# First product of a state-space block with an MLP: two units at a time in seven block products, the scan cut into small pieces between them

## Chip, cores and metric

The kernel runs on one core of one Trainium2 chip. The metric is the device time in microseconds of one execution of the whole program; the time of a version is the median of several executions. Engines are named as in the profile: PE (TensorE matmul), PEld (its weight loads), DVE (VectorE), ACT (ScalarE), POOL (GpSimd), SP (SyncE, which only issues DMAs here).

## What is computed

A Mamba-2 scan over 4 batches, 8 heads, 768 positions, head size 32 and state size 16, and behind it, per token, a two-layer MLP with Silu. The reference, cut:

```python
log_a = np.log(np.clip(a, 1e-06, 1.0))
for c in range(nc):                                   # chunks in time
    L = np.exp(cum[..., :, None] - cum[..., None, :]) * causal
    M = np.einsum('bhin,bhjn->bhij', Cc, Bc) * L
    y = np.einsum('bhij,bhjd->bhid', M, xc) + np.einsum('bhin,bhnd->bhid', Cc, state) * np.exp(cum)
    state = decay_full * state + np.sum(Bx * decay_from_j, axis=2)
x = y.transpose(0, 2, 1, 3).reshape(3072, 256)
h = x @ w_in                                          # 3072x256 by 256x2048
out = (h / (1 + exp(-h))) @ w_out                     # 3072x2048 by 2048x256
```

Everything is fp32, except that the two weight matrices arrive as 64-bit floats and are converted on the chip.

## The kernel before, in words

**Units.** The 3072 tokens are 12 units of 256 (UT), three per batch. Each unit goes through the scan, then the first product (`f_s1`), then the second (`f_s2`).

**The scan of a unit** is a chain of pieces. `f_P` (L237) clips the decays of the unit and scans them on DVE (tile pfx); `f_E` (L264) does the same for the 64-by-64 decay table E, one DVE scan over 1024 columns. `f_T` (L277) transposes B and C on PE into a PSUM tile and ACT copies them out (bh, and ce twice with masks); `f_C` (L294) multiplies C by pfx on DVE (cw); `f_B` (L271) multiplies B by E's last column, on POOL in the loop (BT). `f_G` (L297) runs the small matmuls of the chunk states and of C by B into the four PSUM banks of tile gy; DVE multiplies by E (M), then ACT copies the states out (dm). `f_S` (L334) chains the states on DVE (st). `f_Y` (L352) runs the small matmuls of y into gy again, and ACT copies them to XM, the transposed input of the MLP.

**The first product**, `f_s1(g, j)`, j from 0 to 7, makes two of the 16 feature blocks: four block products of 128x128 weights by 128x256 tokens into one PSUM bank (tile hp, two buffers), and one Silu over 512 columns on ACT into gT. **The second product**, `f_s2(g, j)`, makes four products for half c = j // 4 of the unit's output rows into tile o_ps (two buffers); after 16 of them ACT copies the half out and SP stores it in two DMAs. Every block product stands in the trace as two PE records, each with its weight load.

**The order** is written out by hand; engines run their own instructions in that order and wait on each other only for data and buffers. In the start (L424 to L486) the scans of units 0 to 2, the conversion of the 16 weight pieces and the first products of units 0 and 1 are interleaved. A piece n is loaded into a ring of 8 raw buffers, `w_size` (ACT), `w_bits` (DVE, then POOL) and `w_sign` (DVE) convert it, and the sign step issues the load of piece n + 8. `busy(n)` (L192) runs n products of zeros on PE. Then the loop (L487) over g = 2 to 13 does in each of eight steps j: four first products of unit g, a piece of the scan of unit g + 1, four second products of unit g - 2. The last two rounds have second products only. `load_unit` puts the loads of a later unit on SP's queue.

Tiles of the scan come from pool `sc` (two buffers each), loads from `loads` (three). PSUM has eight banks: four for gy, two for hp, two for o_ps. Two accesses of different engines to one bank of a tile are put one behind the other.

## Time and profile before

| | us |
|---|---|
| runs shown | 399.66, 400.35, 400.27 |
| median | 400.27 |
| profiled execution, its own time | 399.42 |
| its span, first to last instruction | 397.7 |
| PE busy | 384.8 |
| DVE, ACT, POOL busy | 114.5, 116.1, 32.7 |
| first products (L388), 768 records, busy | 180.9 |
| second products (L399), 768 records, busy | 180.7 |

The span is what the trace shows; 1.72 us of the execution lie around it. "Busy" of PE counts overlapping records once, and matmul ends are modelled, so a cost per product is better read from the chain of waits, where each piece ends when the next begins. In a row of grouped instructions stand line, engine, operation, out<-in, shapes and count, then busy us and mean ns of one, then the idle time of the engine just before them and what ended it. In a row of the timeline stand start and duration in us, and the idle time before in brackets.

### The profile page before, as it was taken

The numbers are of one execution on the slowest core, as the hardware profiler recorded it, in microseconds if no ns is written. First come the engines' busy times: TensorE is split into PE (matmuls) and PEld (weight loads), VectorE is DVE, ScalarE is ACT, GpSimd is POOL, SyncE is SP. The second block draws the span as 40 slices with busy tenths as digits, with TensorE's granted clock in tenths as the row PEclk, the third lists the DMA queues.
The fourth block names the chain that finished last, engine by engine and source line by source line (L and its number), as shares of the span: only waits on it lengthen the run. The fifth ranks groups of instructions, "written<-read, shape, count | busy, mean of one in ns | idle before, by whom it ended". The sixth has DMA issues, their size and how long they took to land.

```text
span 397.7 us, 7960 instructions
## 1 busy us (share of the span) xinstructions
PE 384.8 (97%) x3477; PEld 323.3 (81%) x3477; DVE 114.5 (29%) x211; ACT 116.1 (29%) x250; POOL 32.7 (8%) x38
## 2 busy tenths in 40 slices
PE   8779899999999999999999999999999999999995
PEld 3447788888888888888888888888888888888884
DVE  7763988660600500410420330240150110000000
ACT  2445756223313222322322322321322222221000
POOL 2222356200000000000000000000000000000000
PEclk9899999999999999999999999999999999999999
DMA  9999399405403502601700700900900000000101
GB/s 153 198 283 232 132 191 126 45 2 93 51 5 80 56 16 58 76 15 41 93 15 25 109 15 14 119 15 8 128 13 2 15 13 2 15 13 7 21 13 26
DMA packets 105966, 25.18 MB, mean 63 GB/s; under 512 B 97228, under 2 KB 101836, under 8 KB 105932
## 3 DMA queue, kind: packets, MB, share of 16 engines
q1 hardware_dynamic: 103716, 24.42, 34.5%
q10 hardware_dynamic: 2216, 0.26, 0.5%
q8 instruction: 27, 0.44, 0.5%
q14 instruction: 7, 0.06, 0.1%
HBM read 21.52 MB, written 3.15 MB: 62 GB/s over the span
## 4 chain that ended last, share of the span: by engine, by line
PE 92%; DVE 3%; ACT 1%; DMA 1%; issue 1%; ACTq 0%; DVEq 0%
PE o_ps L399 43%; PE hp L388 40%; PE gy L371 2%; PE gy L317 2%; PE gy L362 2%; DMA bct<-in_B_dram 1%; PE gy L309 1%; PE hp L282 1%; PE hp L195 1%; DVE E L248 1%; DVE w_in_sb L159 1%; DVE wu L151 0%; ACT wu L143 0%; DVE st L348 0%; DVE pa L240 0%
## 5 line engine op out<-in xcount | busy, mean ns | idle before, releaser
L388 PE MATMUL hp<-XM,w_in_sb 128*128 128x256 f32 x768 | 180.9, 380 | 4.3 <-DVE w_in_sb L159 2.0
L399 PE MATMUL o_ps<-w_out_sb,gT 128*128 128x256 f32 x768 | 180.7, 381 | 0.0
L388 PEld LDWEIGHTS hp<-XM,w_in_sb 128*128 128x128 f32 x768 | 145.3, 190 | 26.0 <-DVE w_in_sb L159 2.2
L399 PEld LDWEIGHTS o_ps<-w_out_sb,gT 128*128 128x128 f32 x768 | 143.7, 190 | 20.8 <-issue 1.5
L390 ACT ACTIVATE gT<-hp 128x512 f32<-128x512 f32 x96 | 57.4, 598 | 189.3 <-PE hp L388 189.3
L295 DVE TENSOR_TENSOR cw<-hp,pfx 128x256 f32<-128x256 f32 x12 | 5.1, 424 | 150.7 <-ACT ce L291 150.7
L154 POOL TENSOR_TENSOR wv<-wu,wv 128x512 uint32<-128x512 uint32 x16 | 23.5, 1470 | 44.6 <-DVE wu L153 29.3
L274 POOL TENSOR_TENSOR BT<-bct,E 128x256 f32<-128x256 f32 x10 | 6.6, 658 | 216.8 <-DVE E L248 216.8
L404 ACT ACTIVATE o_sb<-o_ps 128x256 f32<-128x256 f32 x24 | 9.2, 384 | 49.7 <-PE o_ps L399 49.7
L321 DVE TENSOR_TENSOR M<-gy,E 128x1024 f32<-128x1024 f32 x12 | 14.7, 1225 | 29.7 <-PE gy L317 29.7
L248 DVE TENSOR_TENSOR_SCAN E<-ab,diag 128x1024 f32<-128x1024 f32 x10 | 22.9, 2292 | 0.8
L329 ACT ACTIVATE dm<-gy,par 128x64 f32<-128x64 f32 (+1 forms) x48 | 10.9, 311 | 21.4 <-DVE M L321 21.4
L151 DVE TENSOR_SCALAR wu<-wu 128x512 f32<-128x512 f32 x16 | 13.1, 820 | 9.8 <-ACT wu L143 9.8
L348 DVE SCALAR_TENSOR_TENSOR st<-st,pfx,dm 128x64 f32<-128x64 f32 x40 | 12.5, 312 | 6.6 <-ACT dm L329 4.9
L362 PEld LDWEIGHTS gy<-cw,st 32*64 32x64 f32 x352 | 6.6, 135 | 6.6 <-issue 3.3
L195 PE MATMUL hp<-idle 128*128 128x512 bf16 x29 | 9.1, 448 | 1.9 <-DVE idle L190 1.3
L145 ACT ACTIVATE wv<-raw 128x512 f32<-128x512 uint32 x16 | 10.9, 678 | 0.0
L143 ACT ACTIVATE wu<-raw 128x512 f32<-128x512 f32 x16 | 10.8, 678 | 0.0
L371 PE MATMUL gy<-M,xt 64*32 64x64 f32 x768 | 10.6, 231 | 0.0
L362 PE MATMUL gy<-cw,st 32*64 32x64 f32 x352 | 8.4, 229 | 2.2 <-ACT wu L143 1.2
L377 ACT ACTIVATE XM<-gy 128x512 f32<-128x512 f32 x12 | 7.2, 597 | 11.1 <-PE gy L371 11.1
L291 ACT ACTIVATE ce<-hp,par 128x256 f32<-128x256 f32 x24 | 10.1, 480 | 0.0
(45 smaller groups left out, 113.0 us busy)
## 6 DMA issues: line engine op xcount, KB each, us to landing
ab<-in_a_dram SPq DMA_DIRECT2D x40, 128.0 KB
raw<-in_moe_w_in_dram SPq DMA_DIRECT2D x8, 512.0 KB
raw<-in_moe_w_out_dram SPq DMA_DIRECT2D x8, 512.0 KB
xt<-in_x_dram SPq DMA_DIRECT2D x24, 128.0 KB
out_dram<-o_sb SPq DMA_DIRECT2D x48, 64.0 KB
bct<-in_C_dram SPq DMA_DIRECT2D x24, 64.0 KB
pa<-in_a_dram SPq DMA_DIRECT2D x11, 128.0 KB
bct<-in_B_dram SPq DMA_DIRECT2D x22, 64.0 KB
```

The lines of the kernel that those rows point to most:

```text
L145: nc.scalar.activation(v, raw[n][:, :, :, 0], AF.Copy, scale=2.0 ** -51, bias=2.0)
L151: nc.vector.tensor_scalar(out=wu[n], in0=wu[n], scalar1=LEAST, scalar2=MOST, op0=ALU.max, op1=ALU.min)
L154: nc.gpsimd.tensor_tensor(out=v, in0=u, in1=v, op=ALU.add)
L195: nc.tensor.matmul(out=t, lhsT=idle[:, 0:128], rhs=idle, start=True, stop=True)
L248: nc.vector.tensor_tensor_scan(out=E[u][:, k:k + n].rearrange("p k h t -> p (k h t)"), data0=t, data1=diag[:, 0:n * H].rearrange("p g t -> ...
L321: nc.vector.tensor_tensor(out=M[u].rearrange("p k g x -> p g k x"), in0=gram[:, :, 0:256].rearrange("p g (k x) -> p g k x", k=2), in1=E[u] ...
L348: nc.vector.scalar_tensor_tensor(out=o, in0=ST[u][:, t], scalar=PFX[u][:, Q * t + Q - 1:Q * t + Q], in1=dm[:, k, c], op0=ALU.mult, op1=ALU ...
L362: nc.tensor.matmul(out=y[64 * q:64 * q + 64, 2 * w + c, 64 * k:64 * k + 64], lhsT=sp[32 * g:32 * g + 32, t], rhs=cw[32 * g:32 * g + 32, Q ...
L371: nc.tensor.matmul(out=y[32 * q:32 * q + 32, 2 * w + c, 64 * k:64 * k + 64], lhsT=xc[64 * c:64 * c + 64, k, h], rhs=m[64 * c:64 * c + 64, ...
L388: nc.tensor.matmul(out=hp[:, i], lhsT=w_in_sb[:, kc, f * 128:(f + 1) * 128], rhs=xm[:, kc], start=(kc == 0), stop=(kc == KC - 1))
L390: nc.scalar.activation(GTS[g][:, 2 * j:2 * j + 2], hp, AF.Silu)
L399: nc.tensor.matmul(out=OPS[g], lhsT=GTS[g][:, f, 128 * c:128 * c + 128], rhs=w_out_sb[:, f, :], start=(f == 0), stop=(f == NF - 1))
```

## The change

**First products from unit 4 on.** Units 2G and 2G + 1 (G from 2 to 5) and feature blocks 2j and 2j + 1 are taken as a 2-by-2 block product with an inner size of two blocks. That is eight block products; `f_x1` does it in seven, after Strassen in Winograd's form. Four sums of weight blocks (SW) are made once on POOL by `f_SW`, four sums of token blocks (XT) per pair on DVE by `f_XT`; both lie in buffers of the raw ring, which has 7 buffers in place of 8. Three PSUM tiles X, W and Y are used per step (hp, three buffers). X collects P1, then P6, P7 and a fourth product on top of each other; between these ACT copies P1 and U2 out, DVE adds from it into gT, and at last ACT takes Silu of it. DVE does three additions per step, ACT three copies and four Silus of 256 columns. The sums lie in gT and Silu is taken there in place.

**Second products** come from a generator (`s2_list`), one product at a time, two units behind in pairs: 1, 3, 3 and 1 per step between the first products. Both halves of a unit lie in one bank (o_ps, one buffer in place of two); ACT copies them out together, 512 columns, but in the last two units half by half.

**The scan** is cut into smaller functions. From unit 6 on `scan_plan` spreads the scans of the next pair's two units over the eight steps: DVE and ACT pieces go between the additions and Silus of `f_x1`, PE's pieces behind it. E is scanned in four pieces, M in two; BT moves to DVE there. The transposes go to a bank of gy in place of hp. Pool `sc` has one buffer (pfx, st and the copies two).

**The start.** `f_Ab` uses hp and `busy` uses o_ps. One `busy(4)` is gone, two are `busy(3)`; `f_S(0)` comes ahead of the first weight steps; for unit 1 `f_C` comes ahead of `f_B` and both ahead of `w_bits(3)`. Unit 3's round of the loop now holds the scans of units 4 and 5.

```diff
-    rawp = ctx.enter_context(tc.tile_pool(name="rawp", bufs=8))
+    rawp = ctx.enter_context(tc.tile_pool(name="rawp", bufs=7))
-    sc = ctx.enter_context(tc.tile_pool(name="sc", bufs=2))
+    sc = ctx.enter_context(tc.tile_pool(name="sc", bufs=1))
-    ps_h = ctx.enter_context(tc.tile_pool(name="ps_h", bufs=2, space=bass.MemoryType.PSUM))
-    ps_o = ctx.enter_context(tc.tile_pool(name="ps_o", bufs=2, space=bass.MemoryType.PSUM))
+    ps_h = ctx.enter_context(tc.tile_pool(name="ps_h", bufs=3, space=bass.MemoryType.PSUM))
+    ps_o = ctx.enter_context(tc.tile_pool(name="ps_o", bufs=1, space=bass.MemoryType.PSUM))
...
-        tp = ps_h.tile([128, 4, 128], FP32, name="hp")
+        tp = ps_s.tile([128, 4, 512], FP32, name="gy")[:, 0]
...
+    def s2_list(units, apart=False):
+        for g in units:
+            o = ps_o.tile([128, 2, d_model], FP32, name="o_ps")
+            o_sb = opool.tile([128, 2, d_model], FP32, name="o_sb")
+            b, t0 = at(g)
+            for c, f in [(c, f) for c in range(2) for f in range(NF)]:
+                nc.tensor.matmul(out=o[:, c], lhsT=GTS[g][:, f, 128 * c:128 * c + 128], rhs=w_out_sb[:, f, :],
+                                 start=(f == 0), stop=(f == NF - 1), skip_group_check=True)
+                if f == NF - 1 and (apart or c == 1):
+                    cs = slice(c, c + 1) if apart else slice(0, 2)
+                    nc.scalar.activation(o_sb[:, cs], o[:, cs], AF.Copy)
...
+                yield
...
+        a0, a1, op = ((wj[:, 0, 1], wj[:, 1, 1], ALU.add), (SW[0], wj[:, 0, 0], ALU.subtract),
+                      (wj[:, 0, 0], wj[:, 0, 1], ALU.subtract), (wj[:, 1, 0], SW[min(i, 1)], ALU.subtract))[i]
+        nc.gpsimd.tensor_tensor(out=t, in0=a0, in1=a1, op=op)
...
+        a0, a1 = ((b1[:, 0], b0[:, 0]), (b1[:, 1], t[:, 0]), (b1[:, 1], b1[:, 0]), (b0[:, 1], t[:, 1]))[i]
+        nc.vector.tensor_tensor(out=t[:, i], in0=a0, in1=a1, op=ALU.subtract)
...
+    def f_x1(G, j, dve, act):
...
+        X, W, Y = (ps_h.tile([128, 512], FP32, name="hp")[:, 0:UT] for _ in range(3))
...
+        mm(X, wj[:, 0, 0, j], b0[:, 0])
+        p1 = copy("p1", X)
+        mm(W, wj[:, 1, 0, j], b0[:, 1])
+        add(g0[:, 2 * j], W, p1)
+        f_s2(1)
+        mm(Y, SW[0][:, j], t[:, 0])
+        p5 = copy("p5", Y)
+        mm(X, SW[1][:, j], t[:, 1], False)
+        u2 = copy("u2", X)
+        silu(g0[:, 2 * j], g0[:, 2 * j])
+        other(dve, 3)
+        other(act, 3)
+        f_s2(3)
+        mm(X, SW[2][:, j], t[:, 2], False)
+        add(g1[:, 2 * j + 1], X, p5)
+        silu(g1[:, 2 * j + 1], g1[:, 2 * j + 1])
+        f_s2(3)
+        mm(X, wj[:, 1, 1, j], t[:, 3], False)
+        silu(g0[:, 2 * j + 1], X)
+        other(dve, 2)
+        mm(Y, SW[3][:, j], b1[:, 1], False)
+        add(g1[:, 2 * j], Y, u2)
+        silu(g1[:, 2 * j], g1[:, 2 * j])
+        other(dve, 1)
+        other(act, 9)
+        f_s2(1)
...
+            plan[j][0].extend([partial(f_P0, u), partial(f_P1, u), E0[0], E0[1], E1[0], E1[1]])
+            plan[j][2].append(partial(f_T0, u))
+            plan[j + 1][0].extend([E1[2], E1[3], partial(f_C, u), partial(f_B, u, nc.vector)])
+            plan[j + 1][1].extend([partial(f_T1, u), partial(f_T2, u, 0), partial(f_T2, u, 1)])
+            plan[j + 1][2].append(partial(f_G, u))
+            plan[j + 2][0].extend([partial(f_M, u, 0), partial(f_M, u, 1), lambda: None, partial(f_S, u, 0, 2),
+                                   partial(f_S, u, 2, 4)])
+            plan[j + 2][1].extend([partial(f_D, u, 0), partial(f_D, u, 1)])
+            plan[j + 2][2].append(partial(f_Y, u))
+            plan[j + 3][1].append(partial(f_X, u))
...
+    for G in range(2, NU // 2):
+        S2.append(s2_list((2 * G - 2, 2 * G - 1)))
+        plan = scan_plan(G + 1) if G + 1 < NU // 2 else [([], [], []) for _ in range(8)]
+        for j, (dve, act, pe) in enumerate(plan):
+            f_x1(G, j, dve, act)
+            for what in pe:
+                what()
...
+    S2.append(s2_list((NU - 2, NU - 1), True))
+    f_s2(64)
```

## The prediction, made before the result was known

> **What bounds the kernel now.** I read the page from the top: busy times, the 40 slices, the chain that ended last.

> ```profile
> span 397.7 us, 7960 instructions
> PE 384.8 (97%) x3477; PEld 323.3 (81%) x3477; DVE 114.5 (29%) x211; ACT 116.1 (29%) x250; POOL 32.7 (8%) x38
> ...
> PE   8779899999999999999999999999999999999995
> ...
> PE 92%; DVE 3%; ACT 1%; DMA 1%; issue 1%; ACTq 0%; DVEq 0%
> ```

> TensorE is busy from the second slice to the last but one, and 92% of the chain is its work. "Busy" is no proof, so I went to the groups of instructions, shapes kept apart, between 66 and 344 us, where the loop over units runs:

> ```profile
> L399 PE MATMUL o_ps<-w_out_sb,gT 128*128 128x256 f32 x580 | 139.0, 382 | 0.0
> L388 PE MATMUL hp<-XM,w_in_sb 128*128 128x256 f32 x576 | 136.1, 379 | 0.0
> ```

> The last column is idle time before the group: 0.0. Nothing that another engine does is late there. The chain of waits cut to one unit gives the true cost of a product, free of the overlap in "mean ns":

> ```profile
> 158.36 0.44 PE hp L282 x4
> ...
> 162.25 0.38 PE gy L309 x32
> 162.64 0.62 PE gy L317 x32
> 163.26 1.92 PE o_ps L399 x8
> 165.18 1.73 PE hp L388 x8
> ...
> 173.82 0.51 PE gy L362 x24
> 174.32 0.79 PE gy L371 x53
> ...
> 189.12 0.44 PE hp L282 x4
> ```

> Every block product is two records, so eight records are four products: 1.73 / 4 = 0.432 us. The unit repeats after 189.12 - 158.36 = 30.76 us, which is 64 products (27.65) and 3.1 of scan (0.44 + 0.38 + 0.62 + 0.51 + 0.79, and twice 0.19 where 1.92 stands for 1.73). So in the loop time is the count of products, and a product removed is worth 0.432 us as long as no wait takes its place.

> **Term 1, the products.** From unit 4 on, a step of two units does 7 first products instead of 8; 4 pairs x 8 steps = 32 products: 32 x 0.432 = **-13.8 us**. The second product and the scan keep their counts, and the last two units' second products run alone at the end as before. SP gets two stores per unit instead of four, and loads two units ahead as before; DMA holds 1% of the chain, so I cost this at nothing.

> **Term 2, does a step hold together?** Its PE order is X W s Y X sss X sss X Y s (s: one second product), 15 slots of 0.432 = 6.48 us, and bank X is read by another engine four times. The price of a hand-off:

> ```profile
> 257.12 0.93 ACT L329 ACTIVATE dm<-gy,par 128x64 f32<-128x64 f32 x4 [1.74 <-DVE M L321]
> ...
> 262.48 1.70 PEld L399 LDWEIGHTS o_ps<-w_out_sb,gT 128*128 128x128 f32 x8
> 262.69 1.89 PE L399 MATMUL o_ps<-w_out_sb,gT 128*128 128x256 f32 x8
> 262.89 0.60 ACT L390 ACTIVATE gT<-hp 128x512 f32<-128x512 f32 x1 [1.29 <-PE hp L388]
> ```

> The next product starts at 262.69, the reader of the last one at 262.89: 0.20 us behind the slot's end. The weight load of a run goes out 0.21 ahead of it (262.48). The readers' own times:

> ```profile
> L390 ACT ACTIVATE gT<-hp 128x512 f32<-128x512 f32 x96 | 57.4, 598 | 189.3 <-PE hp L388 189.3
> ...
> L329 ACT ACTIVATE dm<-gy,par 128x64 f32<-128x64 f32 x40 | 9.5, 314 | 21.4 <-DVE M L321 21.4
> L404 ACT ACTIVATE o_sb<-o_ps 128x256 f32<-128x256 f32 x24 | 9.2, 384 | 49.7 <-PE o_ps L399 49.7
> ...
> L295 DVE TENSOR_TENSOR cw<-hp,pfx 128x256 f32<-128x256 f32 x12 | 5.1, 424 | 150.7 <-ACT ce L291 150.7
> ```

> so 0.384 for a copy or Silu of 256, 0.424 for an addition with one PSUM input; and ACT overlaps neighbours by 0.1, four dm of 0.314 in 0.93. When a wait does bite, PE loses more than the wait, since the weight load is no longer hidden; the early part shows it:

> ```profile
> 20.88 0.04 issue
> 20.93 2.01 PE hp L388 x8
> ```

> 0.04 us to PE, and 2.01 for 1.73: 0.28 more. Walking through the step: P1 is copied by 0.43 + 0.20 + 0.38 = 1.01, and X is written again at 1.73. U2 is copied by 2.74, needed at 3.45. The addition from X ends at 4.51, needed at 5.18. The last Silu from X ends at 5.61 + 0.20 + 0.384 + 0.04 = 6.23 and the next step writes X at 6.48, with its weight load 0.21 earlier, at 6.27: 0.04 spare. This is the only tight place. The scan pieces fit, by the windows' row of almost one unit (PE, PEld, DVE, ACT, POOL):

> ```profile
> 190.00:220.00 30.00, 30.00 (x288) 25.71 (x288) 6.87 (x13) 7.24 (x17) 0.64 (x1) 1.00 0.28 43
> ```

> DVE's whole scan is 6.87; if half of it fell into one step, 3.4 + 3 x 0.424 = 4.7 is still under 6.48. ACT's share beside eight Silus is 7.24 - 8 x 0.598 = 2.5 per unit, and seven short activations are 2.7 per step. So: 0 if the 0.04 holds, 0.1 x 32 = 3.2 if ACT is a tenth late; I take 0.03 per step, **+1.0 us**, near the end that the rows name.

> **Term 3, one bank for the second product.** o_ps goes from two buffers to one, which holds both halves of a unit, so the first product of a unit waits for the copy of the unit before. That copy stands in ACT's queue behind the last Silu of the step, which waits for DVE's addition, which waits for slot 13: 6.05 + 0.20 + 0.42 + 0.38 + 0.60, with three hand-overs of 0.03 to 0.04, is 7.75, or 1.27 in the next step. There two first products (0.86) come ahead of the waiting one. Loss: 0.41, and 0.28 to restart, less 0.1 as ACT's neighbours overlap: 0.6. This happens after step 7 of all pairs but the last (3 times) and after step 3 of the last pair (once): 2.4. After step 3 of the other three pairs the four transposes (0.44) fill most of it: 0.2 each, 0.6. After the last step nothing is ahead: 1.27 + 0.28 = 1.55. In the tail, where halves are copied apart, 0.20 + 0.38 + 0.04 + 0.28 = 0.9 at each of three boundaries (half to half, unit to unit, half to half): 2.7. The half-to-half ones wait only if PE may not write columns of a bank that ACT reads elsewhere. dm's row above says that it may not: dm reads other columns than M and yet waits for M every time, 21.4 us in all. Sum **+7.3 us**; bounds 4 (half-to-half free, the boundaries in pairs hidden by half) and 8.3 (0.1 more at about ten of the eleven). The cover that is relied on is two first products; without it each boundary in a pair would cost 0.86 more, as after the last step.

> [...]

> **Term 4, the first 35 us**, where latency counts and not the products. Here the order changes: the transposes go to the scan's own banks, hp has three buffers, four idle products ahead of unit 0's third step and two elsewhere go, S moves ahead of the first weights' steps, C ahead of B.

> ```profile
> 8.57 0.47 PE L309 MATMUL gy<-xt,BT 64*32 64x64 f32 x32
> ...
> 8.86 0.42 DVE L295 TENSOR_TENSOR cw<-hp,pfx 128x256 f32<-128x256 f32 x1 [0.34 <-ACT ce L291]
> ...
> 22.63 0.69 DVE L245 TENSOR_TENSOR_SCAN pfx<-pa,pb 128x256 f32<-128x256 f32 x1
> ...
> 23.24 0.40 DVE L274 TENSOR_TENSOR BT<-bct,E 128x256 f32<-128x256 f32 x1
> ...
> 23.61 1.02 PE L195 MATMUL hp<-idle 128*128 128x512 bf16 x4 [0.69 <-ACT gT L390]
> ...
> 26.61 0.45 PE L309 MATMUL gy<-xt,BT 64*32 64x64 f32 x32
> ```

> ```profile
> 34.63 10.63 PE L388 MATMUL hp<-XM,w_in_sb 128*128 128x256 f32 x48 [0.69 <-ACT XM L377]
> ```

> Unit 1's G starts at 26.61, behind the third step, which stood behind idle products that waited for a bank. With P, C and B back to back on DVE (22.63 + 0.69 + 0.42 + 0.40) and the third step started as soon as its weights are there, G can start at 24.2: 2.4 earlier. Against that, unit 0's G must wait for C (8.86 + 0.42 = 9.28) instead of B: 0.75 later, of which the first weights' DVE steps pass on 0.5. **-1.9 us**; what follows up to the loop is one chain through ACT and DVE that starts from unit 1's first step (34.63) and moves with it. Bounds -2.5 (nothing given back) and 0 (the weights' chain on DVE paces it). The raw ring of 7 instead of 8 buffers sends the eighth piece out behind unit 2's loads, where the ninth stood:

> ```profile
> 33.02 18.83 SPq L135 DMA_DIRECT2D raw<-in_moe_w_out_dram  x8
> ...
> 40.61 0.69 ACT L143 ACTIVATE wu<-raw 128x512 f32<-128x512 f32 x1
> ```

> It goes out at 33.0 and is first read at 40.6, the eighth of these steps, so 7.6 us cover it: nothing. Were they not enough, ACT, DVE and the first products behind it would wait for the rest.

> **Term 5, GpSimd.** Four differences of 128x1024 are put there in unit 2's last steps.

> ```profile
> 77.56 0.64 POOL L274 TENSOR_TENSOR BT<-bct,E 128x256 f32<-128x256 f32 x1 [5.19 <-DVE E L248]
> ...
> 83.10 0.20 DVE L346 COPY st<-dm 128x64 f32<-128x64 f32 x1 [0.65 <-ACT dm L329]
> ...
> 83.52 0.93 DVE L348 SCALAR_TENSOR_TENSOR st<-st,pfx,dm 128x64 f32<-128x64 f32 x3 [0.22 <-ACT dm L329]
> ...
> 88.16 0.58 PE L362 MATMUL gy<-cw,st 32*64 32x64 f32 x24
> ```

> At 0.64 per 256 elements one takes 2.56, so they run from 78.2 to 88.4 on this clock, across unit 3's state updates (83.1 to 84.5), which Y needs at 88.16. And GpSimd does hold up such updates:

> ```profile
> 13.57 2.01 DVE L348 SCALAR_TENSOR_TENSOR st<-st,pfx,dm 128x64 f32<-128x64 f32 x3
> 13.59 1.27 POOL L154 TENSOR_TENSOR wv<-wu,wv 128x512 uint32<-128x512 uint32 x1 [10.12 <-DVE st L346]
> ```

> Three updates beside a GpSimd operation took 2.01 where three alone took 0.93. If the last updates come only after the fourth difference, Y ends 1.3 late; if they slip in before it, 0. I take **+0.5 us**. [...]

> **Sum.** -13.8 + 1.0 + 7.3 - 1.9 + 0.5 = -6.9. The profiled execution took 399.42 us, 1.72 outside its span of 397.7; -6.9 makes it 392.5 (span 390.8). The median of the runs is 0.85 above that execution, so the forecast is 400.27 - 6.9 = **393.4 us**.

> **Rivals.**

> *The one bank costs less.* If PE may write one half while ACT reads the other (-1.8) and X's hand-over never bites (-1.0): 400.27 - 9.7 = 390.6. For it: the 0.04 spare; against: dm's wait. With the early bound, and the pair boundaries hidden by half, 388.5.

> *Slower: X comes back late in every step.* The place is the last Silu from X, with 0.04 spare. If it takes the 598 ns of the row for 512 columns in place of 384, X is free 0.21 later, 0.17 too late in each of 32 steps, 5.4 us; if it also stands 0.15 behind a neighbour in ACT's queue, 0.32 x 32 = 10.2, and 400.27 - 13.8 + 10.2 + 7.3 - 1.9 + 0.5 = 402.6. It decides from 0.25 per step on, where the 7.9 that are left of the gain are used up. Against it: L404 reads 256 columns from PSUM in 384 ns.

> *The early gain is not there and steps lose 0.1:* 400.27 - 13.8 + 3.2 + 7.3 + 0 + 1.3 = 398.3.

> *The change doesn't do what it says:* nothing saved because PE is held by something else than its products. The 0.0 idle time speaks against; it would come out near 400.3.

> **Chances.** Forecast as summed (391.5 to 395.5) 0.50; the bank costs less 0.23; early gain missing or steps a little late 0.14; no change 0.05; slower 0.08. Range 388.5 to 398.5: from the first rival's end to the third, leaving out the last two. A difference of 0.2%, 0.8 us, is about what a measurement of this kernel can tell. Faster by more 0.87, within it 0.05, slower 0.08.

> **What would show it.** Right: 704 records of first products in place of 768; a pair of units with scan after some 58.9 us (15 x 8 x 0.432 = 51.8, 6.2 of scan, 0.8 of waits) against 61.5; o_ps idle of about 7 us, put down to ACT's o_sb, in place of 0.0; unit 1's first step near 32.7 us instead of 34.6; DVE updates of unit 3 over 1 us long. Wrong: idle time at first products waiting for gT or p1 in every step; a wait for o_ps after step 3 of every pair; the early part unmoved.

## The result

The changed kernel takes **390.91 us** (median of 4, 390.89 to 390.97) against 399.97 for the kernel before beside it (median of 4): ratio 0.9774, 95% interval 0.9757 to 0.9791, 9.1 us faster. The forecast was 393.4 with a range of 388.5 to 398.5. The profiled execution took 390.89, its span 389.2 in place of 397.7. The page of the changed kernel:

```profile
span 389.2 us, 8176 instructions
PE 372.1 (96%) x3407; PEld 309.8 (80%) x3407; DVE 166.4 (43%) x371; ACT 158.8 (41%) x400; POOL 38.1 (10%) x36
...
PE   7869989999999999999999999999999999998985
```

DVE and ACT do some 50 and 40 us more work, and PE is still the one that is full. The groups of PE between 126 and 302 us, the three pairs with scan (columns as before: busy, mean ns, idle before):

```profile
L447 PE MATMUL o_ps<-w_out_sb,gT 128*128 128x256 f32 x384 | 99.0, 380 | 0.5 <-ACT o_sb L451 0.5
L502 PE MATMUL hp<-raw 128*128 128x256 f32 x144 | 38.9, 379 | 0.0
L502 PE MATMUL hp<-XM,w_in_sb 128*128 128x256 f32 x97 | 26.3, 392 | 0.0
L502 PE MATMUL hp<-XM,raw 128*128 128x256 f32 x48 | 14.3, 379 | 0.0
L502 PE MATMUL hp<-raw,w_in_sb 128*128 128x256 f32 x48 | 14.3, 379 | 0.0
```

No first product (L502, four kinds by where weights and tokens lie) waits: 0.0. The only idle time is at the second product, for the copy of o_ps. Over the whole span these are PE's waits:

```profile
PE hp L434 <- DVE w_in_sb L163: 5.0, 4, 2.0
PE o_ps L447 <- ACT o_sb L451: 3.5, 8, 1.1
```

The first row is the start: unit 0's four steps, each waiting for its weights. The kernel before has one such wait, of 2.0 us. The second row is the one bank, eight times, 3.5 us; each restart costs more on top: in the place below its weight load starts together with its product, both at 184.71 us. One place in a pair, from the chain of waits, and the tail from the timeline:

```profile
184.08 0.59 ACT o_sb L451
184.67 0.04 issue
184.71 0.70 PE o_ps L447 x2
```

```profile
361.19 1.03 PE L447 MATMUL o_ps<-w_out_sb,gT 128*128 128x256 f32 x4
362.69 1.13 PE L447 MATMUL o_ps<-w_out_sb,gT 128*128 128x256 f32 x4 [0.47 <-ACT o_sb L451]
```

Two records take 0.70 in place of 0.43 after the copy. In the tail, between one half of a unit and the next, 1.50 us pass from the start of four records to the start of the next in place of 0.86.

### The profile page after: what moved, and what is told of

It is laid out like the page before. It is cut to its first block, busy times and chain, and to the rows that moved or that the text cites. A ratio compares the mean times of both kernels' runs of the same rounds, so it can differ in the third digit from the quotient of the medians.

```text
span 389.2 us, 8176 instructions
## 1 busy us (share of the span) xinstructions
PE 372.1 (96%) x3407; PEld 309.8 (80%) x3407; DVE 166.4 (43%) x371; ACT 158.8 (41%) x400; POOL 38.1 (10%) x36
## 4 chain that ended last, share of the span: by engine, by line
PE 91%; DVE 2%; ACT 2%; POOL 2%; DMA 1%; issue 1%; ACTq 0%; POOLq 0%; DVEq 0%
PE o_ps L447 43%; PE hp L502 25%; PE hp L434 14%; PE gy L414 2%; PE gy L350 2%; PE gy L405 2%; POOL wv L158 1%; PE gy L305 1%; PE gy L342 1%; DMA bct<-in_B_dram 1%; ACT o_sb L451 1%; DVE w_in_sb L163 1%; DVE M L359 1%; DVE wu L157 0%; PE o_ps L199 0%
## 5 line engine op out<-in xcount | busy, mean ns | idle before, releaser
L505 DVE TENSOR_TENSOR gT<-hp,p 128x256 f32<-128x256 f32 x64 | 27.2, 425 | 102.0 <-PE hp L502 54.5
L434 PE MATMUL hp<-XM,w_in_sb 128*128 128x256 f32 x256 | 61.0, 388 | 5.7 <-DVE w_in_sb L163 5.0
L508 ACT ACTIVATE gT<-gT 128x256 f32<-128x256 f32 x96 | 39.9, 415 | 51.0 <-DVE gT L505 51.0
L434 PEld LDWEIGHTS hp<-XM,w_in_sb 128*128 128x128 f32 x256 | 48.7, 193 | 13.9 <-DVE w_in_sb L163 3.0
L502 PE MATMUL hp<-raw 128*128 128x256 f32 x192 | 51.9, 379 | 0.0
L516 ACT ACTIVATE p<-hp 128x256 f32<-128x256 f32 x64 | 24.6, 385 | 48.0 <-PE hp L502 47.9
L502 PEld LDWEIGHTS hp<-raw 128*128 128x128 f32 x192 | 36.5, 190 | 5.0
L436 ACT ACTIVATE gT<-hp 128x512 f32<-128x512 f32 x32 | 19.1, 597 | 44.3 <-PE hp L434 44.3
L502 PE MATMUL hp<-XM,w_in_sb 128*128 128x256 f32 x128 | 34.1, 389 | 0.0
L502 PEld LDWEIGHTS hp<-XM,w_in_sb 128*128 128x128 f32 x128 | 22.9, 190 | 3.9 <-issue 1.0
L262 DVE TENSOR_TENSOR_SCAN E<-ab,diag 128x256 f32<-128x256 f32 (+1 forms) x28 | 24.9, 908 | 0.6
L502 PE MATMUL hp<-XM,raw 128*128 128x256 f32 x64 | 19.0, 379 | 0.0
L502 PE MATMUL hp<-raw,w_in_sb 128*128 128x256 f32 x64 | 19.0, 379 | 0.0
```

What stands on the lines that cost most here:

```text
L262: nc.vector.tensor_tensor_scan(out=E[u].rearrange("p k h t -> p (k h t)")[:, Q * g0:Q * (g0 + n)], data0=t, data1=diag[:, 0:n].rearrange(" ...
L434: nc.tensor.matmul(out=hp[:, i], lhsT=w_in_sb[:, kc, f * 128:(f + 1) * 128], rhs=xm[:, kc], start=(kc == 0), stop=(kc == KC - 1))
L436: nc.scalar.activation(GTS[g][:, 2 * j:2 * j + 2], hp, AF.Silu)
L502: nc.tensor.matmul(out=o, lhsT=w, rhs=x_, start=start, stop=True, skip_group_check=True)
L505: nc.vector.tensor_tensor(out=o, in0=p, in1=q, op=ALU.add)
L508: nc.scalar.activation(o, i, AF.Silu)
```

## The experiments

The edits are to the changed kernel. Profiled spans are compared with its 389.2; the medians come with those of the kernel before on the same chip.

**The products alone.** Eight block products per step, Silu straight from the banks, all else of the change in place:

```diff
         mm(X, wj[:, 0, 0, j], b0[:, 0])
-        p1 = copy("p1", X)
-        mm(W, wj[:, 1, 0, j], b0[:, 1])
-        add(g0[:, 2 * j], W, p1)
+        mm(X, wj[:, 1, 0, j], b0[:, 1], False)
+        silu(g0[:, 2 * j], X)
...
```

> The new kernel with eight block products per step in place of seven, four Silus straight from the banks, no additions and no copies; everything else of the change stays. Theory (PE is held by its products, so the change is worth 32 x 0.432 = 13.8 us and the rest of it costs): 390.9 + 13.8, less some 1.2 because the copy of o_ps no longer stands behind an addition, 403.5 us, slower than the kernel before by about 3.5. Rival (most of the gain comes from the new order of the scan and of the second products): between 391 and 397 us. 768 records of first products either way.

401.96 us, ratio 1.003 (1.0 to 1.0059), span 399.4. So all else of the change together gains nothing, and the seven products are the gain. Against 389.2 the span is 10.2 longer. Two things have to be added back. This profile lacks a stretch of half clock in the start that the changed kernel's has (see below): in the chain of waits its second products begin at 60.65 us in place of 62.15, 1.5 us. And it has fewer waits for o_ps in the loop and a shorter one at the tail's entry, as the row shows:

```profile
PE o_ps L447 <- ACT o_sb L451: 2.3, 4, 0.7
```

Four waits, all at the tail, in place of eight; with restarts, and by the lengths of the steps and of the tail, that is about 2.0 us. 10.2 + 1.5 + 2.0 = 13.7, against 13.8 for 32 products.

**Is the last Silu from X near the path?** One more copy of X ahead of it:

```diff
+        copy("u2", X)
         silu(g0[:, 2 * j + 1], X)
```

> In each of the 32 steps ACT copies X once more, unused, ahead of the last Silu from X. Theory of the tight place (X free at 6.23 of the 6.27 us at which the next step's weight load goes out): the copy takes 0.27 to 0.38 of ACT ahead of the Silu, so each step is 0.2 to 0.35 late, 7 to 11 us in all, 398 to 402 us, with idle time at the first product of each step put down to ACT. Rival (there is room, the zero idle time is far from its edge): 391 to 392 us.

390.49 us (389.94 to 391.14), ratio 0.9736 (0.9677 to 0.9795), span 389.2: nothing. The rival holds. The timeline of one step's end:

```profile
320.09 0.59 PE L502 MATMUL hp<-XM,raw 128*128 128x256 f32 x2
...
320.29 0.38 ACT L516 ACTIVATE u<-hp 128x256 f32<-128x256 f32 x1 [0.85 <-PE hp L502]
...
320.57 0.38 ACT L508 ACTIVATE gT<-hp 128x256 f32<-128x256 f32 x1
...
320.95 0.81 PE L502 MATMUL hp<-XM,w_in_sb 128*128 128x256 f32 x3
```

The copy took 0.28, the Silu ended at 320.95, and the next step's first product began at 320.95, on its beat (320.09 + 2 x 0.43). With the 0.04 us that a release takes it would have been late if it used this bank, so the pool must have given it another one of the three. How far the edge is, three copies were to show:

> Three unused copies of X, not one, ahead of the last Silu from X in each step. Theory A (the place is near the path after all, only one slot of 0.43 further than forecast, since the second and not the first product of the next step takes that bank): three copies take 3 x 0.28 = 0.84 us, spare was 0.47, so each step is about 0.4 late at its second product, 32 x 0.4 = 12 us, some 403 us. Theory B (this bank is not waited for before the next step's fifth slot, 1.7 us later): 391 us.

392.17 us, ratio 0.9785 (0.9749 to 0.9822), span 390.8, and no step waits at a first product. In one step of its trace the last Silu from X runs from 322.37 to 322.78, and by then the next step's first and second product have begun (322.16 and 322.59). So neither of them uses this bank, and Theory B holds. The 1.6 us all lie at the copies of o_ps, which now stand behind more ACT work: eight places of 0.19 to 0.20 each:

```profile
PE o_ps L447 <- ACT o_sb L451: 4.4, 8, 1.3
```

**Do the small pieces matter?** P and E whole, ahead of the second addition:

```diff
-            plan[j][0].extend([partial(f_P0, u), partial(f_P1, u), E0[0], E0[1], E1[0], E1[1]])
+            plan[j][0].extend([partial(f_P, u), partial(f_E, u), lambda: None])
...
```

> From unit 6 on the scans P and E run as one piece each, both ahead of the step's second addition, as large as in the kernel before; nothing else changes. Theory (the small pieces are what keeps DVE's additions on time): P and E take 0.65 + 0.69 + 0.74 + 2.29 = 4.4 us behind the first addition, which ends at 1.5, so the second addition ends at 6.3 in place of 4.5 and the product that waits for it comes 1.1 us and 0.1 of restart late, 6 times (units 6 to 11): 7 us, 398 us. Rival (DVE is busy under half of the time, so the size of the pieces doesn't matter): 391 to 392 us.

398.25 us, ratio 0.9924 (0.9898 to 0.995), span 396.6: 7.4 us lost, as the theory had it. Its wait and one of its places:

```profile
PE hp L502 <- DVE gT L505: 5.6, 6, 1.3
```

```profile
190.37 2.29 DVE L262 TENSOR_TENSOR_SCAN E<-ab,diag 128x1024 f32<-128x1024 f32 x1
...
192.58 0.40 DVE L505 TENSOR_TENSOR gT<-hp,p 128x256 f32<-128x256 f32 x1
...
193.03 0.70 PE L502 MATMUL hp<-raw,w_in_sb 128*128 128x256 f32 x2 [0.79 <-DVE gT L505]
```

The addition stands behind one scan of 2.29 us, and the product that writes the same bank behind the addition. DVE is busy under half the time in both kernels; what counts is the longest piece ahead of a short one that PE needs.

**GpSimd twice over.**

```diff
-        nc.gpsimd.tensor_tensor(out=t, in0=a0, in1=a1, op=op)
+        for _ in range(2):
+            nc.gpsimd.tensor_tensor(out=t, in0=a0, in1=a1, op=op)
```

> GpSimd makes each of the four weight sums twice over, so its stretch of 2.36 us operations grows from 9.4 to 19 us. Theory (each state update of unit 3 can be held up by a whole GpSimd operation, and the updates now end 0.1 us behind the start of Y): with four more operations behind, the second and third update wait for one each, the updates end about 4.5 us later, and PE waits 4 us at Y of unit 3: 395 us, the wait put down to st. [...]

391.73 us, ratio 0.9767 (0.9719 to 0.9815), span 389.5. In this profile, too, the half clock is missing (first second product at 60.59 us in the chain of waits, 1.6 earlier), so the edit cost about 0.3 + 1.6 = 1.9 us. The timeline, first of the changed kernel, then of this one:

```profile
82.67 2.36 POOL L479 TENSOR_TENSOR raw<-w_in_sb 128x1024 f32<-128x1024 f32 x1
82.93 2.14 DVE L383 COPY st<-dm 128x64 f32<-128x64 f32 x1 [0.67 <-ACT dm L369]
84.98 2.36 POOL L479 TENSOR_TENSOR raw<-w_in_sb,raw 128x1024 f32<-128x1024 f32 x1
85.17 2.88 DVE L385 SCALAR_TENSOR_TENSOR st<-st,pfx,dm 128x64 f32<-128x64 f32 x3
...
87.90 0.58 PE L405 MATMUL gy<-cw,st 32*64 32x64 f32 x24
```

```profile
81.37 2.25 DVE L383 COPY st<-dm 128x64 f32<-128x64 f32 x1 [0.67 <-ACT dm L369]
83.72 7.08 DVE L385 SCALAR_TENSOR_TENSOR st<-st,pfx,dm 128x64 f32<-128x64 f32 x3
...
86.34 0.46 PE L405 MATMUL gy<-cw,st 32*64 32x64 f32 x16
88.43 0.34 PE L405 MATMUL gy<-cw,st 32*64 32x64 f32 x8 [1.63 <-DVE st L385]
```

In the changed kernel the copy takes 2.14 us in place of 0.20 and three updates 2.88 in place of 0.93. The copy ends at 85.07, the first update at 87.41, each just behind the end of a GpSimd operation (85.03 and 87.34); no further GpSimd operation follows, the other two updates are short, and Y doesn't wait. With twice the operations every update is held up, and Y waits 1.6 us and a restart. The mechanism is shown, its size was half of what was expected: the last update is for the next unit, and this Y doesn't need it.

**The tail in banks of its own.**

```diff
+            if apart:
+                o = [ps_h.tile([128, 512], FP32, name="hp")[:, 0:d_model]... for _ in range(2)]
...
```

> The last two units' second products go, half by half, into the three banks of hp, which nothing else uses by then. Theory (entry 1.36 and three boundaries of 0.74 to 0.79 are waits for the one bank): 390.9 - 3.6 = 387.3 us, the tail without gaps. Rival (the gaps are ACT's or the stores', not the bank's): 390 to 391 us.

386.84 us, ratio 0.9638 (0.9606 to 0.967), span 385.6: 3.6 us faster, to the tenth. The tail is one run, 128 records at 0.216:

```profile
353.84 27.79 PE L451 MATMUL hp<-w_out_sb,gT 128*128 128x256 f32 x128
```

**Room at the boundaries in the pairs.**

```diff
-        f_s2(1)
         mm(Y, SW[0][:, j], t[:, 0])
         p5 = copy("p5", Y)
+        f_s2(1)
...
         add(g1[:, 2 * j], Y, u2)
+        other(dve, 1)
+        f_s2(1)
         silu(g1[:, 2 * j], g1[:, 2 * j])
-        other(dve, 1)
         other(act, 9)
-        f_s2(1)
```

> In every step the first second-product moves behind the product into Y, and the step's last second-product, with the copy of o_ps behind it, comes ahead of the last Silu in ACT's queue. Theory (four boundaries in the pairs cost 0.49 us each because the copy stands behind addition and Silu and has two products of cover): the copy ends near 0.8 in the next step, the waiting product stands at 1.30, so 2.0 us go and nothing comes back: 388.9 us. Rival (the moved copy makes P1's copy or the Silu late and the wait only changes its place): 390.5 to 392 us.

387.7 us, ratio 0.9662 (0.9631 to 0.9692), span 386.5: 2.7 us, the 2.0 of the pairs' boundaries, the small losses after step 3 (0.2) and 0.4 at the tail's entry, where the copy also comes earlier. Four waits for o_ps are left, in the tail:

```profile
PE o_ps L447 <- ACT o_sb L451: 2.2, 4, 0.7
```

**The clock in the start.** Unit 1's G starts at 24.89 in the changed kernel (26.61 before) and its wait for weights ends at 28.02 (29.67 before); then it loses what it gained. Changed kernel, then kernel before:

```profile
28.02 3.30 PE L434 MATMUL hp<-XM,w_in_sb 128*128 128x256 f32 x8 [2.05 <-DVE w_in_sb L163]
31.12 1.45 PE L199 MATMUL o_ps<-idle 128*128 128x512 bf16 x4
...
34.67 1.56 PE L434 MATMUL hp<-XM,w_in_sb 128*128 128x256 f32 x6 [0.69 <-ACT XM L423]
```

```profile
29.67 1.99 PE L388 MATMUL hp<-XM,w_in_sb 128*128 128x256 f32 x8 [1.99 <-DVE w_in_sb L159]
31.50 1.03 PE L195 MATMUL hp<-idle 128*128 128x512 bf16 x4
...
34.63 1.56 PE L388 MATMUL hp<-XM,w_in_sb 128*128 128x256 f32 x6 [0.69 <-ACT XM L377]
```

Eight records take 3.30 in place of 1.99. The windows tell why (behind the length of each stands PE's busy time; the granted clock is the third figure from the end):

```profile
25.14:28.55 3.41, 1.36 (x65) 0.99 (x42) 2.70 (x6) 1.17 (x5) 1.26 (x1) 1.00 1.24 151
28.55:31.97 3.42, 3.42 (x9) 2.15 (x8) 0.76 (x3) 0.61 (x2) 0.00 (x0) 0.50 0.61 59
```

The clock is granted at half for one window of 3.41 us, behind one in which PE was busy for 1.36. The edit fills the gap:

```diff
     f_GMD(1)
+    busy(7)
     w_sign(3)
```

> Seven products of zeros are put behind unit 1's G, where PE stands idle from 26.1 to 28.0 us. Theory (the early gain of 1.65 us is there at 28.0 and is lost in the 3.4 us at half clock that follow the idle stretch): the clock stays at 1.0, the eight records at 28.0 take 2.0 in place of 3.3, unit 1's first step starts near 33.0 in place of 34.67, and the whole is 1.6 us faster: 389.3 us. Rival 1 (the half clock comes whatever PE does there): 390.9. Rival 2 (the chain through ACT and DVE behind it takes the gain back, as its own pace is set by DVE): unit 1 starts early, but the second products start at 62 as before, 390.9.

389.7 us (389.37 to 389.84), ratio 0.9711 (0.9683 to 0.974), span 387.7, 1.5 faster than the changed kernel's profile. Eight records at 28.23 take 1.99, unit 1 starts at 33.19. Both rivals fall for the profile that was taken. But two of the other profiles kept the clock without this edit, so the changed kernel ran again:

> The changed kernel once more, nothing edited, beside the others. Theory (the half-clock window in the start comes or not by where a free-running 3.4 us window falls on the idle stretch of PE): its executions fall into two groups, near 390.9 with the window and near 389.3 without. Rival (it comes always, and what kept it away from two of the other kernels was their edit): all within 390.5 to 391.2.

390.92, 390.06, 389.56, 389.89, 389.95, 389.65 us: median 389.92, ratio 0.9729 (0.9698 to 0.976). The profiled one is the 390.92, and has the half clock, from 28.86 us in place of 28.55; the other five are 0.9 to 1.4 faster. The mean granted clock is on record for all six: 0.996 for the 390.92, which is one window of 3.41 us at half in 389.2, and 1.0 for the other five. So the two groups of the theory are there: with nothing edited the half clock came in one execution of six and stayed away in five. With the filler all six had 0.999 or 1.0.

The kernel before is touched by it too. Its 19 executions beside the eight products were 398.73 and 399.24 us at a clock of 1.0 and 0.999, 399.55 to 400.28 at 0.995 or 0.996, and 402.0 to 403.12 at 0.986 to 0.990. So at full clock on both sides the kernels are about 9.1 us apart (398.99 and 389.89), an estimate from two executions of the one and five of the other on another chip. With the kernel before at 0.995 or 0.996 and the changed one at 0.996, on one chip, they are 9.0 apart (median 399.90, and 390.92).

**All three edits together.**

> The three edits together: banks of hp in the tail, the moved second product and copy in the steps, seven products of zeros in the start. Theory (they act in three separate places and add up): 390.9 - 3.6 - 2.0 - 1.6 = 383.7 us. Rival (one of them only moves a wait): as the sum of what the three show alone, at most 387.3 if only the tail's is real.

383.75 us (383.49 to 384.47), ratio 0.9567 (0.9539 to 0.9595), span 382.2: the best version, 7 us ahead of the changed kernel in the profile. Alone they gave 3.6, 2.7 and 1.5; the 0.4 at the tail's entry is in two of them, so 7.4 was to be had. The 0.4 that is missing lies in the start: in the chain of waits the second products begin at 61.09 us here and at 60.72 with the filler alone. PE waits for o_ps nowhere:

```profile
L451 PE MATMUL o_ps<-w_out_sb,gT 128*128 128x256 f32 x640 | 162.3, 380 | 0.0
```

## Why the prediction was right, point by point

The span fell by 8.5 us where 6.9 were forecast; the medians by 9.1.

- **Products, -13.8.** Right: 704 records in place of 768 (256 in single units, 448 in pairs), and 13.7 by the experiment with eight products. A pair with scan takes 58.71 us (184.71 to 243.42), forecast 58.9.
- **Steps, +1.0.** Nothing was lost. The sum put 0.04 us of spare at the last Silu from X, on the assumption that the next step's X lies in the same bank. It doesn't, and three copies, which put that Silu off by 0.81, brought no wait there. The forecast of the second addition's place was right, as the whole scan showed: 7.4 us lost for 7 expected.
- **One bank, +7.3.** The mechanism was right in each of its places: in the tail PE waits 0.47 us (to 362.69) for ACT's copy of the other half, other columns of the same bank, and with the halves in banks of their own it waits nowhere in the tail. The size was too large: 3.6 for the tail and its entry (4.25 forecast) and 2.3 in the pairs (3.0), 5.9 in all. The profile counts 3.5 of it as idle time, from the modelled end of a record on, where about 7 was named as the sign. Each boundary lost 0.1 to 0.2 less than reckoned, and the restart is the part that was too large. From half to half of the tail 7.64 to 7.70 us pass from start to start, against 6.91 for 32 records: 0.64 of wait in the first, near the forecast 0.62, and 0.10 of restart in place of 0.28. The 0.28 came from the chain of waits, where a piece runs to the end of its last record, while the waits were reckoned from slot to slot.
- **Start, -1.9.** The profiles show 1.65 of gain at 28 us (28.02 for 29.67) and keep 0.3 of it at the first second product (62.15 for 62.41 in the chain of waits). The step that failed is "moves with it": a window at half clock follows and costs what had been won, and unit 1's first step starts at 34.67, where 32.7 was named as the sign. The clock was not among the terms. Nor is the 1.65 the new order's alone, since the profile of the kernel before has a half-clock window of its own, from 14.74 us, on its chain:

```profile
14.99 0.81 PE gy L362 x16
15.80 1.11 PE gy L371 x61
16.92 1.59 PE hp L195 x4
...
23.61 1.04 PE hp L195 x4
```

  The four idle products alone took 1.59 in place of 1.04, and with the small matmuls ahead of them, set against such matmuls later in the start (0.62 for 32, 0.80 for 53), the window cost that chain about 1.1 us, an estimate. So the new order is worth some 0.5 to 1 us by these figures, not 1.9: 1.65 - 1.1 is the lower, and the upper is what 13.8 - 5.9, and 0.2 to 0.3 at the last store, leave of the 9.1 at full clock. No profile of the kernel before at full clock is there to settle it. Whether the half clock at 28 us comes from the idle products that were taken out stays open, too: the kernel before has a wait of 1.99 us at the same place, and a window from 27.60 to 31.01 would hold only 1.43 us of its PE work; in its profile the windows lay otherwise, with 2.71 and 2.14.
- **GpSimd, +0.5.** 0 in place of 0 to 1.3. Copy and updates are held up as forecast (2.14 and 2.88 us), and those that Y needs end before it gets to them.

Summed as the two profiles have it: -13.8 + 0 + 5.9 - 0.3 + 0 = -8.2, and the last store ends 0.2 to 0.3 earlier behind its copy. That the total came near the forecast is in part luck: the steps and GpSimd cost 1.5 less than reckoned and the bank 1.4 less, and the start gave 1.6 less in this pair of profiles. The rival that the bank costs less was the nearest in number (390.6), but its reason was not: PE does wait from half to half. The slower rival, X late in every step, would have needed 0.25 us per step, and three copies (0.81) were not enough for it.

## What to carry to other kernels

Where one engine is full and waits for nothing, count its instructions: the 32 products taken away here were worth their time, 13.7 us, though DVE got half as much work again (166.4 us for 114.5). Then look for what was paid to make room for it, here a buffer less, and for a place where another bank lies idle at that very time. On an engine with time to spare the size of the longest piece still matters if something short stands behind it that the full engine needs (P and E whole, 2.29 us the longest, ahead of an addition of 0.40 cost 7.4 us). And before a gain or loss of one or two us in a start is put down to an edit, compare executions with the same granted clock: with nothing edited, one at 0.996 and five at 1.0 were 0.9 to 1.4 us apart here.

## What the runs showed of the hardware

In these profiles the half clock in the start came as one stretch of 3.41 us, and its place was not the program's alone: with the same kernel it began at 28.55 us in one profile and at 28.86 in another, and it stayed away in five of the six executions that were run later. In the kernel before, the clock was at half from 14.74 to 18.15 us and again from 397.03 us to the end of the span; the 378.88 us between are 111 times 3.413, as windows of this length side by side would give. Eight windows of the start were followed by one at half clock: PE was busy 1.36 us in the changed kernel's (1.36 to 1.40 in the seven profiles with its start that have one, whose mean clocks are 0.993 to 0.996), and 1.46 in the kernel before at 11.33. Two at about 26.3, in the profiles with eight products and with GpSimd's sums twice, had 1.50 and 1.51 and were not. No other window of the first 76 us held less than 1.93 in the changed kernel's profile or 2.13 in that of the kernel before, and none of these was followed by half clock. One of each:

```profile
11.33:14.74 3.41, 1.46 (x13) 0.53 (x11) 2.13 (x4) 2.85 (x8) 1.15 (x1) 1.00 0.96 147
14.74:18.15 3.41, 3.16 (x84) 2.03 (x85) 3.26 (x7) 1.19 (x3) 1.15 (x2) 0.50 0.82 113
```

```profile
26.25:29.66 3.41, 1.51 (x7) 1.36 (x8) 2.98 (x7) 0.93 (x4) 0.90 (x1) 1.00 0.85 104
29.66:33.08 3.42, 2.71 (x102) 1.73 (x101) 0.86 (x2) 2.32 (x4) 0.65 (x1) 1.00 1.00 133
```
